# One attention-plus-MoE kernel: the route of its first loads, the written order of its first steps, and the form of its slot table

## The chip, the cores and the metric

The kernel runs on one core of a Trainium2 chip. The metric is device time in microseconds (us), the median of several executions. Before the change it is 366.8 us (three runs, 366.43 to 367.79). The profile was taken in an execution of its own, of 357.85 us, whose span from first to last instruction is 356.3 us. Sums of durations are made against that span.

The engines are TensorE (PE, with its weight loads listed as PEld), VectorE (DVE), ScalarE (ACT), GpSimd (POOL) and SyncE (SP). DMAs are issued by SP, ACT and POOL.

## The reference

There are two stages. The second takes the rows of the first.

```
q_n = q / sqrt(mean(q*q) + 1e-6) * g_q          # per row of 64, likewise k_n
attn = softmax(q_n @ k_n^T / 8)                 # 8 batches, 12 heads, 448 tokens
x = (attn @ v)  as rows [3584, 768]
e(row) = token_id * 2654435761 % 8              # expert of each row, from its low 3 bits
out[row] = relu(x[row] @ w1[e]) @ w2[e]         # w1: 8 x 768 x 1024, w2: 8 x 1024 x 768
```

## The kernel before

**Attention.** Two heads make one step, so that a batch has six steps and the whole has 48 (0 to 47). Steps are prepared in groups: batch 0 has groups of one, two and three steps, every later batch two groups of three. Groups are numbered 0 to 16 (0, 1, 2 are batch 0; 3 and 4 are batch 1).

Preparing a group consists of these operations, named as in the written order: `sqq`/`sqk` (squares of q and k, on DVE or, for two of them, ACT), `sumq`/`sumk` (16 matmuls against the identity that fold the squares), `redq`/`redk` (row sums on DVE), `ln` and `er` (on ACT, giving one over the root), `nk:g.h`/`nq:g.h` (DVE multiplies half a group by it), `v` (a DVE copy of v into the tile `v8`, which also has a column of ones).

A step consists of `Tk`/`Tq` (four PE transposes each, into two halves of one PSUM tile `qkT_ps`, of which there is one), `kT`/`qT` (DVE empties each half), `sc:s.j` (scores, j = 0 to 3, into three PSUM tiles), `exp:s.j` (ACT, PSUM to SBUF), `av:s.0` to `av:s.2` (PE, against v8), `rec` and `x` (DVE: reciprocal of the row sums and the product). When a batch is done its x goes to a DRAM scratch.

The order of all these is written out by hand as two strings of tokens: one for everything up to the first score of step 9 and around it, one (`steady`) that is repeated for each later group. Every engine executes its own instructions in the order in which the tokens emit them. An access to a tile waits for the earlier conflicting accesses to that tile in this same emitted order. `spin` tokens are dummy matmuls on a zero tile, `warm`. `zero:n` tokens are memsets of the parts of q, k, v and v8 buffers that no load fills.

**Loads.** POOL's queue carries nearly all loads; each converts fp32 in DRAM to 16 bits in SBUF. A load of q is two DMAs, one of k or v four. Only the first step's q and k (tile `first`, laid over an exp buffer, fp32) go over SP and ACT, q ahead of k. Then POOL issues: the identity; q, k, v of the rest of batch 0; batch 1 in two halves with a memset of `k_bufs[1]` between and one of `q_bufs[1]` behind; batch 2 with a memset of `v_bufs[1]`; the constants of `setup2`; batch 3. Later batches, and the expert weights, are issued from `hooks(s)`, which runs behind `x` of step s-1.

**Slot table.** While attention runs, the rows of experts 0 and 1 get slots. `SIDE[s]` puts small DVE pieces (m1 to m12) behind `x` of step s-1, and `AV_SIDE[s]` puts pieces of PE work, with a DVE piece that reads them, inside the `av` of step s; these use the free end of that step's `av_ps` bank. The table itself is m10a: 28 matmuls, one per column of tokens, each with a 128x32 stationary tile `lo` and a 128x30 moving tile `hi`, all into partitions 0 to 31 of the bank. The result is the index tile `gidx`, used by the row gathers at the end of attention.

**MoE.** Eight experts follow, two GEMMs each, 512 slots per expert; rows are gathered from and scattered to DRAM by POOL. This part is not touched.

Of the kernel before, what the change touches and what calls it, by code (L numbers as in the profile page):

```python
# [11 lines left out]
I32 = mybir.dt.int32  # L12
AF = mybir.ActivationFunctionType
# [6 lines left out]
def kernel(  # L20
# [12 lines left out]
    nc = tc.nc  # L33
# [63 lines left out]
    iota_i = consts.tile([P, P], I32)  # L97
# [10 lines left out]
    hv = consts.tile([P, 2 * HI0, NTC], FP16)  # L108
    lv = consts.tile([P, LO0, NTC], FP16)
# [5 lines left out]
    warm = consts.tile([P, 512], FP16)  # L115
# [12 lines left out]
    def setup2():  # L128
# [30 lines left out]
        G.tensor_copy(tv16[:], tv[:])  # L159
# [69 lines left out]
    with tc.manual_schedule(), \  # L229
# [21 lines left out]
            :, 0:4 * 8 * D].bitcast(FP32).rearrange("p (a n s d) -> p a n s d", a=2, n=1, d=D)  # L251
# [36 lines left out]
        def raw(a, gi):  # L288
            return first[:, a] if gi == 0 else part_of((q_bufs, k_bufs)[a], *groups[gi])
# [82 lines left out]
        excl = rt([P, 2, NTC], BF16, "excl")  # L372
        far = rt([P, NTC], FP32, "far")
        offl = rt([P, 2], FP32, "offl")
        mine = rt([P, 2, NTC], FP32, "mine")
        slot = rt([P, NTC], I32, "slot")
        parts = rt([P, 2, NTC], I32, "parts")
        parts_h = rt([P, 2, NTC], FP16, "parts_h")
        hi = rt([P, 2 * HI0, NTC], FP16, "hi")
        lo = rt([P, LO0, NTC], FP16, "lo")  # L380
        emp = rt([P, 2 * HI0], FP32, "emp")
        pos = rt([P, 2 * HI0], FP32, "pos")
        flat = lambda t: t[:].rearrange("p a c -> p (a c)")

        def m1():
            V.tensor_scalar(out=eid[:], in0=tid32[:, :, 0], scalar1=E - 1, scalar2=None,
                            op0=ALU.bitwise_and)
            V.tensor_copy(eidf[:], eid[:])

        def m2():  # L390
            for e in range(2):
                V.tensor_scalar(out=oh[:, e], in0=eidf[:], scalar1=float(e), scalar2=None,
                                op0=ALU.is_equal)
            V.tensor_tensor_scan(flat(incl), flat(keep), flat(oh), 0.0, op0=ALU.mult, op1=ALU.add)

        def m3():
            V.tensor_scalar(out=far[:], in0=oh[:, 1], scalar1=-3.0 * FAR, scalar2=4.0 * FAR,
                            op0=ALU.mult, op1=ALU.add)
            V.tensor_tensor(out=excl[:], in0=incl[:], in1=oh[:], op=ALU.subtract)
            V.scalar_tensor_tensor(out=far[:], in0=oh[:, 0], scalar=-4.0 * FAR, in1=far[:],  # L400
                                   op0=ALU.mult, op1=ALU.add)

        SP = SL * (D + 1)

        def m4a(av):
            nc.tensor.matmul(av[:, SP:SP + 2], lhsT=emask[:], rhs=incl[:, :, NTC - 1],
                             start=False, stop=True, skip_group_check=True)

        def m4b(av):
            V.tensor_scalar(out=offl[:], in0=av[:, SP:SP + 2], scalar1=float(EARLY),  # L410
                            scalar2=late[:], op0=ALU.max, op1=ALU.mult)

        def m4c(av):
            rank = av[:, SP:SP + 2 * NTC]
            nc.tensor.matmul(rank, lhsT=u128[:], rhs=flat(oh), start=False, stop=False,
                             skip_group_check=True)
            nc.tensor.matmul(rank, lhsT=gmask[:], rhs=flat(excl), start=False, stop=True,
                             skip_group_check=True)

        def m4d(av):  # L420
# [6 lines left out]
        def m5():  # L427
            V.tensor_tensor(out=far[:], in0=mine[:, 0], in1=far[:], op=ALU.add)
            V.tensor_tensor(out=slot[:], in0=mine[:, 1], in1=far[:], op=ALU.add)

        def m6():
# [4 lines left out]
            V.tensor_copy(parts_h[:], parts[:])  # L436
# [4 lines left out]
        def m7():  # L441
            V.tensor_tensor(out=hi[:], in0=hv[:], in1=wide(parts_h[:, 0], 2 * HI0),
                            op=ALU.is_equal)

        def m8():
            V.tensor_tensor(out=hi[:], in0=hi[:], in1=wide(tv16, 2 * HI0), op=ALU.mult)

        def m9():
            V.tensor_tensor(out=lo[:], in0=lv[:], in1=wide(parts_h[:, 1], LO0), op=ALU.is_equal)

        def m10a(av):
            for c in range(NTC):
                nc.tensor.matmul(av[0:LO0, SP:SP + 2 * HI0], lhsT=lo[:, :, c], rhs=hi[:, :, c],
                                 start=False, stop=(c == NTC - 1), skip_group_check=True)

        def m10b(av):
            val = av[0:LO0, SP:SP + 2 * HI0]
            e1, p1 = emp[0:LO0], pos[0:LO0]
            V.tensor_scalar(out=e1, in0=val, scalar1=0.0, scalar2=float(BIG),
                            op0=ALU.is_equal, op1=ALU.mult)  # L460
            V.tensor_copy(p1, val)

        def m11():
            e1, p1 = emp[0:LO0], pos[0:LO0]
            V.scalar_tensor_tensor(out=p1, in0=p1, scalar=float(N // 2), in1=e1,
                                   op0=ALU.add, op1=ALU.add)
            V.tensor_scalar(out=e1, in0=p1, scalar1=float(N // 2), scalar2=-1.0,
                            op0=ALU.is_gt, op1=ALU.mult)

        def m12():  # L470
            by = lambda t, g: t[0:LO0].rearrange("p (e h) -> p e h", e=2)[:, :, g::NL]
            for g in range(NL):
                n = len(range(g, HI0, NL))
                V.tensor_tensor(
                    out=gidx[LO0 * g:LO0 * g + LO0, 0:2 * KT].rearrange(
                        "p (e c) -> p e c", e=2)[:, :, 0:n],
                    in0=by(pos, g), in1=by(emp, g), op=ALU.add)
# [138 lines left out]
        def ones_v8(eng, v8):  # L616
            eng.memset(v8[:, :, 0:3, D:DP], 1.0)
            eng.memset(v8[:, :, 4:7, D:DP], 1.0)
            eng.memset(v8[:, :, 3::4, D:DP], 0.0)
            eng.memset(v8[0:64, :, 3, D:DP], 1.0)  # L620
            eng.memset(v8[64:P, :, 7, D:DP], 1.0)

        def zeros(n):
            return warm[:, None, 0:D].to_broadcast([P, n, D])

        def zero_act(t, n0, n1, slots):
            for p0, s in slots:
                nc.scalar.copy(t[p0:p0 + 64, n0:n1, s, :], zeros(n1 - n0)[p0:p0 + 64])

        def zero(part):  # L630
            V = nc.vector
            if part == 0:
                zero_kv(V, first[:, 1], 0, 1)
                zero_q(V, first[:, 0], 0, 1)
# [5 lines left out]
            elif part == 3:  # L640
                zero_kv(V, v_bufs[0], 0, 2 * HP)
            elif part == 4:
                for v8 in v8_tiles:
                    ones_v8(V, v8)
            else:
                zero_act(k_bufs[0], HP, 2 * HP, ((64, 3), (0, 7)))
                zero_act(q_bufs[0], HP, 2 * HP, ((64, 3), (64, 7)))

        load_q([nc.sync, nc.scalar], first[:, 0], 0, 0, 1)
        load_kv([nc.sync, nc.scalar, nc.sync, nc.scalar], first[:, 1], k, 0, 0, 1)  # L650
        setup()
        nc.vector.memset(warm[:], 0.0)
# [4 lines left out]
        load(1, 0, 3, "kqv")  # L657
        zero_kv(nc.gpsimd, k_bufs[1], 0, 2 * HP)
        load(1, 3, 3, "kqv")
        zero_q(nc.gpsimd, q_bufs[1], 0, 2 * HP)  # L660
# [15 lines left out]
        AV_SIDE = {16: (m4a, m4b), 18: (m4c, m4d), 28: (m10a, m10b)}  # L676
        SIDE = {13: m1, 14: m2, 15: m3, 19: m5, 20: m6, 22: m7, 24: m8, 26: m9, 29: m11, 30: m12}
# [44 lines left out]
        def emit(text, g, s):  # L722
# [12 lines left out]
            zero:2 zero:5 zero:0 sqk:0 zero:1 sqq:0 spin:9 sumq:0 zero:4 redq:0 zero:3 spin:4  # L735
            sumk:0 redk:0 ln:0 sqq:1 gain:0 er:0 nk:0.0 nk:0.1 spin:4 sumq:1 sqk:1 nq:0.0 spin:1
            Tk:0 nq:0.1 spin:1 sumk:1 redq:1 redk:1 ln:1 Tq:0 er:1 kT:0 qT:0 nk:1.0 spin:3 sc:0.0
            nk:1.1 nq:1.1 sc:0.1 nq:1.0 v:0 sc:0.2 exp:0.0 Tk:1 spin:1 Tq:1 sc:0.3 kT:1 exp:0.1
            exp:0.2 qT:1 sqk:2 spin:1 sc:1.0 Tk:2 exp:0.3 kT:2 Tq:2 exp:1.0 av:0.0 sc:1.1 sc:1.2
            qT:2 sqq:2 sumk:2 av:0.1 sc:1.3 exp:1.1 redk:2 sumq:2 exp:1.2 v:1 av:0.2 sc:2.0 v:2  # L740
            sc:2.1 exp:1.3 redq:2 sc:2.2 ln:2 rec:0 x:0 er:2 av:1.0 av:1.1 exp:2.0 exp:2.1 nk:2.0
            av:1.2 exp:2.2 nk:2.1 nq:2.0 nq:2.1 Tk:3 rec:1 sc:2.3 exp:2.3 Tq:3 kT:3 qT:3 x:1
            sqk:3 Tk:4 Tq:4 kT:4 sc:3.0 sc:3.1 qT:4 av:2.0 sumk:3 sqq:3 exp:3.0 redk:3 sc:3.2
            sc:4.0 sumq:3 av:2.1 sqk:4 exp:3.1 redq:3 sc:3.3 Tk:5 v:3 Tq:5 av:2.2 exp:3.2 exp:4.0
            ln:3 sc:4.1 kT:5 exp:3.3 sc:4.2 qT:5 sc:5.0 er:3 rec:2 exp:4.1 sumk:4 x:2 sc:4.3
            nk:3.0 exp:4.2 redk:4 exp:4.3 nk:3.1 nq:3.0 av:3.0 av:3.1 Tk:6 nq:3.1 sc:5.1 exp:5.0
            av:3.2 kT:6 rec:3 Tq:6 qT:6 sc:5.2 exp:5.1 sc:5.3 x:3 sc:6.0 v:4 exp:5.2 Tk:7 kT:7
# [351 lines left out]
```

## Time and profile before

| what | value |
|---|---|
| median time | 366.8 us |
| span of the profiled execution | 356.3 us |
| busy share PE / DVE / ACT / POOL | 94% / 63% / 53% / 49% |
| first `exp` starts | 13.10 us |
| step 9 starts (`exp:9.0`) | 48.73 us |
| last `exp` ends | 172.02 us |
| first MoE GEMM starts | 174.51 us |
| steady spacing of `exp` steps with no wait | 2.82 us |

The busy shares are means over two stages: attention to about 172 us, in which ACT has the exponentials, and the MoE stage behind it, in which PE is busy all the time (30.00 of 30 us in each stretch from 200 to 320 us). An ACT row of the timeline gives the start, the duration of a merged run of instructions and, in brackets, the idle time ahead of it with the engine that ended it.

### The profile page before, as it was taken

How to read it: one execution, taken by the hardware profiler on the slowest of the kernel's cores; microseconds unless marked ns; L12 is line 12 of the kernel's file. 1: busy time of each engine (PE TensorE's matmuls, PEld its weight loads, DVE VectorE, ACT ScalarE, POOL GpSimd, SP SyncE). 2: the span in 40 equal slices, each digit the busy share in tenths (PEclk: the TensorE clock that was granted, in tenths of full speed). 3: DMA queues.
4: the chain of work that ended last, by engine and by line, in shares of the span. 5: the costliest groups of instructions: out<-in, count | busy, mean ns of one | idle time of the engine just before them, and what ended most of it. 6: DMA issues, size and time to landing. Idle time of an engine off the chain costs nothing. (4 is left out here: it accounts for less than half of the span.)

```text
span 356.3 us, 9342 instructions
## 1 busy us (share of the span) xinstructions
PE 334.6 (94%) x3882; PEld 233.2 (65%) x3882; DVE 223.2 (63%) x574; ACT 188.3 (53%) x293; POOL 174.6 (49%) x253
## 2 busy tenths in 40 slices
PE   6888999999999999999898999999999999999992
PEld 3465667677677677765776767767676676766761
DVE  4888799999998999986788753233233223323311
ACT  4598789999998899999432220202211111111210
POOL 8899996564654210003155258736547374303122
PEclk9999899999999999999999999999999999999998
DMA  8999959999999999952479996999999999702012
GB/s 126 150 141 139 178 108 164 231 193 230 194 230 200 221 240 224 236 100 84 114 157 198 273 227 137 264 247 240 257 198 268 231 233 254 253 3 118 31 63 99
DMA packets 54449, 64.60 MB, mean 181 GB/s; under 512 B 22739, under 2 KB 42459, under 8 KB 54020
## 3 DMA queue, kind: packets, MB, share of 16 engines
q0 software_dynamic: 50832, 57.98, 88.1%
q1 hardware_dynamic: 2978, 5.44, 5.2%
q10 hardware_dynamic: 594, 0.56, 0.5%
q8 instruction: 31, 0.51, 0.5%
q14 instruction: 14, 0.11, 0.1%
HBM read 89.29 MB, written 17.30 MB: 299 GB/s over the span
## 5 line engine op out<-in xcount | busy, mean ns | idle before, releaser
L527 ACT ACTIVATE expT<-sc_ps 128x896 bf16<-128x896 f32 x144 | 123.2, 943 | 6.6 <-PE sc_ps L512 6.4
L805 PEld LDWEIGHTS <-h_sb 128*128 128x128 f16 (+1 forms) x512 | 51.2, 104 | 30.2
L805 PE MATMUL o_ps<-w_sb,h_sb 128*128 128x512 f16 (+3 forms) x384 | 66.2, 326 | 0.0
L812 POOL DMA_INDIRECT out_dram<-o_sb,gidx x32 | 32.6, 1020 | 60.6 <-ACT o_sb L811 27.0
L793 ACT ACTIVATE h_sb<-h_ps 128x480 f16<-128x480 f32 (+2 forms) x44 | 21.8, 498 | 72.0 <-PE h_ps L789 67.7
L203 POOL DMA_INDIRECT xg<-x_scratch,gidx x32 | 32.3, 1011 | 55.2 <-issue 35.4
L789 PEld LDWEIGHTS <-w_sb 128*128 128x128 f16 x336 | 44.2, 146 | 15.3 <-issue 1.1
L789 PE MATMUL h_ps<-xT,w_sb 128*128 128x480 f16 x240 | 49.6, 366 | 0.0
L811 ACT COPY o_sb<-o_ps 128x768 f32<-128x768 f32 x16 | 12.8, 798 | 69.1 <-PE o_ps L805 69.1
L795 DVE TENSOR_SCALAR h_sb<-h_ps 128x480 f16<-128x480 f32 x28 | 18.4, 656 | 42.6 <-PE h_ps L789 42.6
L512 PE MATMUL sc_ps<-qT,kT 64*128 64x448 f16 x288 | 42.4, 359 | 2.5 <-DVE qT L504 0.8
L544 PEld LDWEIGHTS <-expT 128*128 128x128 bf16 x864 | 36.5, 98 | 8.1 <-DVE x_sb L577 6.6
L544 PE MATMUL av_ps<-v,expT 128*128 128x65 bf16 x864 | 41.0, 194 | 0.7 <-DVE x_sb L577 0.5
L811 DVE COPY o_sb<-o_ps 128x768 f32<-128x768 f32 (+1 forms) x16 | 15.3, 956 | 35.4 <-PE o_ps L805 31.1
L494 PE MATMUL qkT_ps<-ident,n 128*128 128x128 f16 x384 | 31.0, 220 | 4.1 <-DVE kT L501 2.0
L270 POOL DMA_DIRECT2D kr<-in_k_dram x40 | 25.8, 657 | 14.6 <-DMA qr<-in_q_dram 9.7
L494 PEld LDWEIGHTS <-n 128*128 128x128 f16 x384 | 22.2, 97 | 15.8 <-issue 10.8
L215 DVE COPY xT<-xT_ps 128x768 f16<-128x768 f16 x28 | 15.5, 553 | 25.4 <-PE xT_ps L214 25.4
L320 PEld LDWEIGHTS <-ident 128*128 128x128 f16 x544 | 24.6, 98 | 9.2 <-issue 4.4
L577 DVE TENSOR_TENSOR x_sb<-av_ps,srec 128x448 f16<-128x448 f32 x48 | 29.8, 620 | 1.2
L530 ACT ACTIVATE expT<-sc_ps 128x448 bf16<-128x448 f32 x48 | 28.2, 588 | 1.5 <-PE sc_ps L515 1.5
L270 POOL DMA_DIRECT2D vr<-in_v_dram x40 | 25.9, 668 | 4.8 <-DMA kr<-in_k_dram 4.0
(186 smaller groups left out, 491.3 us busy)
## 6 DMA issues: line engine op xcount, KB each, us to landing
w_sb<-in_moe_w_dram POOLq DMA_DIRECT2D x24, 384.0 KB, 11.3
w_sb<-in_moe_w_dram POOLq DMA_DIRECT2D x8, 768.0 KB, 12.3
x_scratch<-x_sb SPq DMA_DIRECT2D x15, 288.0 KB, 6.1
w_sb<-in_moe_w_dram POOLq DMA_DIRECT2D x2, 1536.0 KB, 24.0
qr<-in_moe_w_dram POOLq DMA_DIRECT2D x8, 384.0 KB, 17.6
kr<-in_k_dram POOLq DMA_DIRECT2D x12, 192.0 KB, 7.8
qr<-in_q_dram POOLq DMA_DIRECT2D x6, 384.0 KB, 7.7
vr<-in_v_dram POOLq DMA_DIRECT2D x12, 192.0 KB, 9.5
```

Source lines behind the costliest of these rows:

```text
L203: nc.gpsimd.indirect_dma_start(out=xg[0:idx.shape[0]], out_offset=None, in_=x_dram[0:rows, :], in_offset=bass.IndirectOffsetOnAxis(ap=idx, ...
L270: eng.dma_start(out=dst[64 * half:64 * half + 64, :, s0:s0 + cnt, :].rearrange("p n s d -> p n (s d)"), in_=runs(t, h0 + hh, 2, n, tok0, s ...
L494: nc.tensor.transpose(T[:, o:o + P], n8[:, a, i, j].rearrange("p h d -> p (h d)"), ident16[:])
L512: nc.tensor.matmul(sc[:, hh, :S], lhsT=kT[64 * hh:64 * hh + 64, P * j:P * j + P], rhs=qT[64 * hh:64 * hh + 64, :], start=True, stop=True)
L527: nc.scalar.activation(expT[:, 2 * j:2 * j + 2, :], sc[:, :, :S], AF.Exp, bias=0.0, scale=1.0)
L530: nc.scalar.activation(expT[:, 6, :], sc[:, 0, :S], AF.Exp, bias=0.0, scale=1.0)
L544: nc.tensor.matmul(av[:, 2 * t + hh, :], lhsT=expT[:, tl(hh, j), P * t:P * t + P], rhs=v8[:, i, 4 * hh + j, 0:D + 1], start=(hh == 0 and t ...
L577: nc.vector.tensor_tensor(out=xs[b][:, :, hp * D:hp * D + D], in0=av[:, :, :D], in1=srec[:, :, None].to_broadcast([P, SL, D]), op=ALU.mult)
L789: nc.tensor.matmul(h_ps[:, :c1 - c0], lhsT=w1v[:, co, fo, :], rhs=xT[:, co, c0:c1], start=(co == 0), stop=(co == CO - 1))
L805: nc.tensor.matmul(o_ps[0:w, d0:d1], lhsT=h_sb[:, fo, col * P:col * P + w], rhs=w2_sb[:, fo, d0:d1], start=(fo == 0), stop=(fo == FO - 1))
L811: (nc.vector.tensor_copy if col % 2 else nc.scalar.copy)(o_sb[0:w], o_ps[0:w])
L812: scat = nc.gpsimd.indirect_dma_start(out=out[:, :], out_offset=bass.IndirectOffsetOnAxis(ap=idx[0:w], axis=0), in_=o_sb[0:w], in_offset=N ...
```

## The change

- The first step's q is loaded by POOL's queue, as its first DMAs, into `q_bufs[0]` with conversion. Its k alone uses SP and ACT and the tile `first`.
- Batch 1 is loaded whole: k, q, v, ten DMAs in place of twenty. The memsets of `k_bufs[1]` and `q_bufs[1]` move from POOL to DVE (`zero:4`, `zero:5`).
- `v8` gets its ones column with three memsets in place of five, each of one column in place of four.
- The two order strings are replaced.
- The slot table's pieces are rewritten (m1 to m14): 16-bit integer slots without a cast, a base added to the offsets in place of the `far` tile, the wide compares halved and one half per step (23 to 28), and two tables (occupied, and position) of 28 matmuls each in steps 29 and 31. Matmul c writes to partition group 32*(c mod 4), four column tiles of the array. Two matmuls with a replicated identity (`rep4`) combine them in step 33.
- `setup2` makes the new constants (`ug`, `base2`, `rep4`); `iota_i` and `warm` are laid over `lo` and `hi`.

```diff
-    hv = consts.tile([P, 2 * HI0, NTC], FP16)
-    lv = consts.tile([P, LO0, NTC], FP16)
+    hv = consts.tile([P, 2 * HI0, NTC], I16)
+    lv = consts.tile([P, LO0, NTC], I16)
+    rep4 = consts.tile([P, 2, NL, LO0], FP16)
...
-        def m10a(av):
-            for c in range(NTC):
-                nc.tensor.matmul(av[0:LO0, SP:SP + 2 * HI0], lhsT=lo[:, :, c], rhs=hi[:, :, c],
-                                 start=False, stop=(c == NTC - 1), skip_group_check=True)
+        def m13a(av, a):
             for c in range(NTC):
+                g = LO0 * (c % NL)
+                nc.tensor.matmul(av[g:g + LO0, SP:SP + 2 * HI0], lhsT=lo[:, :, c],
+                                 rhs=hi[:, a, :, c], start=False, stop=(c >= NTC - NL),
+                                 skip_group_check=True)
...
         def zero(part):
...
+            elif part == 4:
+                zero_kv(V, k_bufs[1], 0, 2 * HP)
+            elif part == 5:
+                zero_q(V, q_bufs[1], 0, 2 * HP)
...
-        load_q([nc.sync, nc.scalar], first[:, 0], 0, 0, 1)
-        load_kv([nc.sync, nc.scalar, nc.sync, nc.scalar], first[:, 1], k, 0, 0, 1)
+        load(0, 0, 1, "q")
+        load_kv([nc.sync, nc.scalar, nc.sync, nc.scalar], first, k, 0, 0, 1)
...
-        load(1, 0, 3, "kqv")
-        zero_kv(nc.gpsimd, k_bufs[1], 0, 2 * HP)
-        load(1, 3, 3, "kqv")
-        zero_q(nc.gpsimd, q_bufs[1], 0, 2 * HP)
+        load(1, 0, HP)
...
-        AV_SIDE = {16: (m4a, m4b), 18: (m4c, m4d), 28: (m10a, m10b)}
-        SIDE = {13: m1, 14: m2, 15: m3, 19: m5, 20: m6, 22: m7, 24: m8, 26: m9, 29: m11, 30: m12}
+        AV_SIDE = {17: (m5a, m5b), 19: (m7a, m7b), 33: (m14a, m14b)}
+        for a in range(2):
+            AV_SIDE[29 + 2 * a] = (lambda av, a=a: m13a(av, a), lambda av, a=a: m13b(av, a))
+        SIDE = {13: m1, 14: m2, 15: m3, 16: m4, 18: m6, 20: m8, 21: m9}
+        for t, m in enumerate((m10, m10, m11, m11, m12, m12)):
+            SIDE[23 + t] = lambda m=m, e=t % 2: m(e)
...
-            Tk:0 nq:0.1 spin:1 sumk:1 redq:1 redk:1 ln:1 Tq:0 er:1 kT:0 qT:0 nk:1.0 spin:3 sc:0.0
+            Tk:0 nq:0.1 sqk:1 kT:0 spin:1 Tq:0 spin:1 sumk:1 qT:0 sc:0.0 redk:1 ln:1 sc:0.1
+            zero:5 er:1 nk:1.0 exp:0.0 sc:0.2 nk:1.1 nq:1.0 spin:5 Tk:1 nq:1.1 spin:1 Tq:1 v:0
...
-            av:3.2 kT:6 rec:3 Tq:6 qT:6 sc:5.2 exp:5.1 sc:5.3 x:3 sc:6.0 v:4 exp:5.2 Tk:7 kT:7
-            Tq:7 qT:7 av:4.0 av:4.1 av:4.2 sc:7.0 sqq:4 exp:5.3 exp:6.0 sc:6.1 sc:6.2 sumq:4
+            qT:6 exp:5.2 sc:5.3 exp:5.3 av:4.2 sc:6.0 Tk:7 Tq:7 sc:6.1 sc:6.2 sqq:4 rec:4 x:4
+            kT:7 qT:7 av:5.0 v:3 exp:6.0 sqk:5 sc:6.3 av:5.1 sumq:4 exp:6.1 av:5.2 sc:7.0 redq:4
```

## The prediction, made before the run

> **What bounds the kernel now.** I read the page first (busy shares), then the table of stretches, ACT's waits and the timeline. The chain of waits shows only the last scatter, so the bound has to be read by stage.
>
> ```profile
> PE 334.6 (94%) x3882; PEld 233.2 (65%) x3882; DVE 223.2 (63%) x574; ACT 188.3 (53%) x293; POOL 174.6 (49%) x253
> ...
> 31.00:38.90 7.90, 6.50 (x99) 4.63 (x97) 6.62 (x16) 5.16 (x9) 7.85 (x12) 0.85 1.21 145
> 38.90:48.73 9.83, 9.14 (x157) 6.29 (x154) 8.15 (x18) 8.48 (x14) 8.93 (x32) 0.95 1.11 171
> ...
> 89.74:98.91 9.17, 9.07 (x166) 6.40 (x163) 9.10 (x23) 9.13 (x15) 5.82 (x10) 1.00 1.51 192
> 98.91:108.84 9.93, 9.44 (x170) 6.71 (x166) 9.69 (x24) 9.31 (x16) 5.91 (x9) 1.00 1.42 227
> 108.84:120.06 11.22, 11.15 (x194) 8.41 (x192) 9.20 (x26) 9.45 (x14) 4.90 (x8) 1.00 1.30 208
> ```
>
> Behind each stretch stand its length and the busy time of PE, PEld, DVE, ACT, POOL. A steady group takes about 9.1 us, and ACT is busy for all of it (9.13 of 9.17); groups that take longer are those in which ACT waits. From 172 us on PE is the bound and no PE row waits for a weight DMA. So a microsecond that ACT no longer waits in attention is a microsecond at the end, and there is nothing to gain elsewhere.
>
> How much is there? A step of `exp` is 2.82 us (starts at 160.42, 163.23, 166.04), `ln` with `er` 0.62, the one square on ACT 1.50. Up to step 9 ACT needs 9 x 2.82 + 3 x 0.62 + 1.5 = 28.8, and takes 13.10 to 48.73 = 35.6: 6.9 us of waits. From there to 172.02 it needs 39 x 2.82 + 12 x 0.62 = 117.4 and takes 123.3: 5.9 us. These 12.8 us are all that the change can work on, besides the start at 13.10.
>
> ```profile
> 38.90 2.54 ACT L527 ACTIVATE expT<-sc_ps 128x896 bf16<-128x896 f32 x3 [2.35 <-PE sc_ps L512]
> 48.73 2.54 ACT L527 ACTIVATE expT<-sc_ps 128x896 bf16<-128x896 f32 x3 [1.07 <-PE sc_ps L512]
> ...
> 34.93 0.91 DVE L361 COPY v<-vr 128x1536 bf16<-128x1536 bf16 x1
> 35.76 0.46 DVE L501 TENSOR_SCALAR kT<-qkT_ps,g_col 128x512 f16<-128x512 f16 x1
> 36.28 0.38 PE L494 MATMUL qkT_ps<-ident,n 128*128 128x128 f16 x4 [1.01 <-DVE kT L501]
> 38.24 1.30 PE L512 MATMUL sc_ps<-qT,kT 64*128 64x448 f16 x6
> ...
> 113.96 1.85 PEld L453 LDWEIGHTS <-lo 128*32 128x32 f16 x28
> 116.26 0.54 ACT L530 ACTIVATE expT<-sc_ps 128x448 bf16<-128x448 f32 x1 [1.49 <-PE sc_ps L515]
> 108.84 0.34 ACT L335 ACTIVATE ss<-ss,eps_col 128x48 f32<-128x48 f32 x1 [0.43 <-DVE ss L331]
> ```
>
> The largest wait (2.35) is one of order: `v:4` holds DVE for 0.91, `kT:7` comes behind it, `Tq:7` is emitted behind `kT:7` on the same tile and waits 1.01, three `av` follow, and only then the scores that ACT wants. The granted clock is also low there (0.85). The last two rows are the slot table: 28 matmuls in series (66 ns each) make ACT wait 1.49; DVE pieces ahead of `redq` make each `ln` wait, 0.2 to 0.7 us a group (70.75, 89.74, 108.84).
>
> **What the Trainium skill says.** "TensorEngine Tiling (Array Packing)", Key Properties: different tiles can execute weight loads and matmuls in parallel. The trace agrees in kind: the eight matmuls of `av:s.2`, two column halves, load their weights in 0.20 us, 25 ns each, against 66 ns in the unpacked table. "DMA: Bandwidth & Descriptors", Issuing engines are not separate DMA queues: SP, ACT and POOL share the same DMA engines; so moving q to POOL buys issue order, not bandwidth. The trace can't separate that. "GPSIMD Engine Reference", Key points: POOL shares its SBUF interfaces with VectorE. It agrees: the v copy under POOL's memset took 0.91, others 0.55. "VectorE: DVE Perf Modes", What auto-detection actually checks: the doubled rate asks for 16-bit tensors, so int16 compares should keep the 0.58 us rate of the fp16 ones; no int16 row is in this trace.
>
> **The change part by part.**
>
> *First loads.*
>
> ```profile
> 0.97 0.20 POOL masks.py:197 MEMSET ident<- 128x128 f16 x1 [0.29 <-POOLq L1083]
> 1.72 0.83 POOL L260 DMA_DIRECT2D qr<-in_q_dram  x1 [0.18 <-issue]
> 4.36 0.69 DVE L308 TENSOR_TENSOR sq_q<-expT 128x512 f16<-128x512 f32 x1 [1.28 <-DMA expT<-in_q_dram]
> 7.25 0.63 ACT L306 ACTIVATE sq_k<-expT 128x512 f16<-128x512 f32 x1 [0.20 <-DMA expT<-in_k_dram]
> 8.74 0.31 ACT L335 ACTIVATE ss<-ss,eps_col 128x16 f32<-128x16 f32 x1 [0.87 <-DVE ss L331]
> ```
>
> On POOL the first q can be issued at about 0.97 and 1.80; POOL's q issues of that size landed 4.4 to 4.7 us later, so q is there at 6.2 (before: 4.36). k, now first on SP and ACT, has its second pieces issued at 1.8 and 4.2 to landing: 6.0 (before 7.25). DVE then: `sqq:0` on fp16 (half the elements of the 0.68 us row, 0.4), nine small memsets (before, fifteen took 1.28; I take 0.8), `zero:4` 0.76, `redq`, `redk` 0.35: 8.5. `ln:0` at 8.5 in place of 8.74. POOL's later issues slip by the two of q, 1.4 us: q of group 1 lands at 3.9 + 4.4 = 8.3, in time for `sqq:1`; its k at 6.3 + 4.0 = 10.3. `sqk:1` stands ahead of `kT:0` on DVE and ends at 11.1, `kT:0` at 11.5; `Tq:0` is now emitted behind `kT:0` and waits for it, 12.0; `sumk:1` (0.63) stands ahead of the first score; `ln:1` and `er:1` (0.6) stand ahead of `exp:0.0` on ACT. So `exp:0.0` starts at about 13.6, a loss of 0.5. Bounds: 12.9 if the loads land a little earlier, 14.6 if POOL's land a microsecond later. `zero:5` (twice the 0.38 row) lies in the wait for `er:1`: nothing.
>
> *Batch 1 whole.* Ten issues fewer at 0.64 (6.4 us) and three memsets (0.73 + 0.73 + 1.68) leave POOL; `setup2` gains about nine small operations (0.2 to 0.5 each, some 2.5 us). No engine waits for a POOL constant, so this is worth nothing by itself, but for the one DMA wait of `sq_k` (0.81 at 27.72), which ends on DVE and not on ACT. What must hold is that whole k lands before `sqk:3` on ACT, at about 24. The queues had moved 0.97, 1.16 and 1.27 MB in the stretches of 8 us to 24; batch 0 and all k of batch 1 are 2.95 MB: 21 to 22 us. In time.
>
> *Order to step 9.* Of the 6.9 us of waits: `exp:1.1` (0.69) stays, as `sc:1.1` is still behind `Tq:2` behind `kT:2` behind `sqk:2`. `ln:2` (0.42) shrinks, since `v:2` (half of a 1.08 us pair) leaves its place ahead of `redq:2`. The 2.35 goes: `Tk:7 Tq:7 sc:6.1 sc:6.2` follow each other and `Tq:7` waits for no `kT`. The 1.07 goes: `exp:8.1` to `8.3` (2 us) now stand between the last `av:7` and `exp:9.0`. For step 6, DVE has 3.5 us of work between `er:3` and `qT:6`, ACT 4.9 us of `exp`: no wait. I keep 2.5 us of 6.9 for what I can't see: step 9 at 13.6 + 28.8 + 2.5 = 44.9, 3.8 us earlier. Bounds: 1 and 6 of waits.
>
> *Slot table and steady order.* Of 5.9 us, 1.5 is the table and about 4.4 the waits at group borders. DVE loses the casts, `far` and the two passes at the end (about 1.5 us), and gains nearly as much by halving wide passes (fixed cost twice); but a border now has at most one piece of 0.1 to 0.35 ahead of it in place of 0.4 to 0.6: I take 2.6 for 4.4. The table is 56 matmuls for 28, in two steps. Packed at 25 ns each half takes 0.7, of which PE's slack (1.85 - 1.49 = 0.4) hides 0.4: 0.6 in all, for 1.5. Unpacked it is 2 x 1.5 = 3.0; fully hidden 0. Sum: 2.6 + 0.6 against 5.9, 2.7 us earlier; between 0.3 and 4.
>
> Sum: 3.8 + 2.7 = 6.5 us earlier at the end of attention, and at the end: 356.3 - 6.5 = 349.8 in the profiled execution. The others were 10 us longer, with no profile to say where; I take the same difference from the median: 366.8 - 6.5 = 360.3.
>
> **The rivals.**
> 1. *The column tiles don't pack.* The slow 66 ns may be the strided weight read, which stays. Then the table costs 3.0 in place of 0.6, and the steady part gives little: 362.5 to 364. For it: the trace shows packing only with 64 columns. Against: there it works.
> 2. *The order gains nothing that can be measured.* Waits removed at one step come back at the next, because PE and DVE are busy 9 of 9.1 us in a steady group and have no room; the start loses 0.5 to 1. Then 365 to 367. Against: up to 48 us both have room (6.5 and 6.6 of 7.9 us).
> 3. *Slower: whole k comes late.* `sqk:3` holds ACT, in order, so each microsecond past 24 is lost. In the crowded stretch at 60 to 80 us POOL's k issues were 1.5 to 2 us apart and landed 7.8 us later. At that pace the last of four from 15.6 lands at 29.4: 5.4 us lost, q behind it, `sqq:3` too. It outweighs the gain if k lands past 32, with the median then at 369. Against: the bytes moved by 24 us, above.
> 4. *The first q late on POOL* is a matter of 1 us and within the range.
>
> **How the numbers follow.** Likeliest 0.60: 360.3, own range 357 to 363. Rival 1, 0.17: 363.3. Rival 2, 0.11: 366. Slower (rival 3 or its like), 0.12: 369. A measurement of this kernel tells about 0.5%, 1.8 us, from no change. Faster 0.77, same 0.11, slower 0.12. The range is 357.0 to 366.0: it leaves out rival 3, and the few cases below 357 in which nearly all 12.8 us of waits go.
>
> **What would show it.** Right: `exp:0.0` between 13 and 14.5; no ACT wait above 1 us between 20 and 45; step 9 near 45; granted clock near 1 there; two runs of 28 table matmuls of about 0.7 us; last `exp` near 165.5; the MoE stage as long as before. Wrong: an ACT wait at `sqk:3` for a DMA, table runs of 1.9 us each, `exp:0.0` past 15, or a MoE stage that grows by what attention gave.

## The result, and the profile after

The changed kernel took 360.77 us in the median (359.99 to 361.48, four runs), the kernel before 366.93 us (366.43 to 367.79, four runs): ratio 0.983, 95% interval 0.980 to 0.986. The predicted time was 360.3.

The profile does not bear out that difference. The profiled execution of the kernel before had a span of 356.3 us, that of the changed kernel 359.7. Three later sessions, on three different chips, put the kernel before at 359.2 to 359.3 us (166 executions, none above 361.7), and the changed kernel, run in two of them, at the same. The first comparison stands as measured, but what the change does has to be read from traces and from the later comparisons.

The busy shares and five stretches of the changed kernel (columns as before: bounds, length, then busy time of PE, PEld, DVE, ACT, POOL):

```profile
PE 334.4 (93%) x3911; PEld 232.4 (65%) x3911; DVE 225.6 (63%) x567; ACT 187.4 (52%) x293; POOL 170.6 (47%) x250
```

```profile
31.00:38.90 7.90, 7.57 (x129) 5.10 (x126) 7.13 (x19) 7.55 (x13) 7.31 (x20) 1.00 1.51 194
38.90:47.32 8.42, 7.61 (x145) 5.66 (x144) 8.20 (x18) 7.57 (x12) 7.81 (x22) 1.00 0.79 142
89.71:99.03 9.32, 9.32 (x168) 6.50 (x164) 9.22 (x25) 9.07 (x14) 5.73 (x9) 1.00 1.51 193
99.03:108.68 9.65, 9.48 (x166) 6.59 (x164) 9.55 (x25) 9.07 (x15) 5.91 (x9) 1.00 1.42 228
108.68:118.68 10.00, 9.80 (x192) 7.18 (x192) 9.38 (x24) 9.19 (x14) 4.36 (x8) 1.00 1.34 203
```

Up to step 9 the order does its work: between 31.00 and 38.90 ACT is busy for 7.55 us, where it was 5.16, and the granted clock is 1.00, where it was 0.85. The stretch with the table is 10.00 us, where it was 11.22. But the two steady stretches together are hardly shorter than before (18.97 us for 19.10).

The timeline of the changed kernel, ACT's waits and what stands behind them:

```profile
13.86 2.51 ACT L533 ACTIVATE expT<-sc_ps 128x896 bf16<-128x896 f32 x3
47.32 2.57 ACT L533 ACTIVATE expT<-sc_ps 128x896 bf16<-128x896 f32 x3 [0.38 <-PE sc_ps L518]
52.72 0.34 ACT L344 ACTIVATE ss<-ss,eps_col 128x48 f32<-128x48 f32 x1 [2.38 <-DVE ss L340]
117.71 0.54 ACT L536 ACTIVATE expT<-sc_ps 128x448 bf16<-128x448 f32 x1 [0.38 <-PE sc_ps L521]
171.45 0.57 ACT L536 ACTIVATE expT<-sc_ps 128x448 bf16<-128x448 f32 x1
...
49.11 2.54 DVE L370 COPY v<-vr 128x1536 bf16<-128x1536 bf16 x1
49.15 2.09 POOL L668 MEMSET xg<- 128x768 f16 x3
52.43 0.25 DVE L340 TENSOR_REDUCE ss<-qkT_ps 128x24 f32<-128x96 f32 x1
...
116.73 0.53 PEld L463 LDWEIGHTS <-lo 128*32 128x32 f16 x28
116.73 0.65 PE L463 MATMUL av_ps<-hi,lo 128*32 128x30 f16 x28
...
174.87 5.04 PE L796 MATMUL h_ps<-xT_e,w_sb 128*128 128x384 f16 x30 [0.98 <-DVE xT_e L224]
222.02 0.49 PE L223 MATMUL xT_ps<-ident,xg 128*128 128x128 f16 x6 [1.42 <-DVE xT L224]
```

Step 9 starts at 47.32 (before 48.73), although the first `exp` starts 0.76 later. Then one wait of 2.38 us takes it back: the copy `v:4`, 0.55 us in other steps, takes 2.54 while POOL runs three memsets, and `redq` stands behind it on DVE. The table packs: 28 weight loads in 0.53 us, ACT's wait 0.38 in place of 1.49. The last `exp` ends at 172.02 in both kernels. The MoE stage (from its first GEMM to the end of the span) takes 184.8 us, before 181.8; PE has waits in it that the kernel before doesn't have (1.42 at 222.02, 0.52 at 214.56, 0.42 at 181.48; the 0.98 ahead of the first GEMM is as before).

Three questions remain: does the change gain, which of its parts cost what it gives, and why is the MoE stage longer?

### The profile page after: what moved, and what is told of

It reads as the page before. It is cut to its first block, busy times and chain, and to the rows that moved or that the text cites. A ratio compares the mean times of both kernels' runs of the same rounds, so it can differ in the third digit from the quotient of the medians.

```text
span 359.7 us, 9392 instructions
## 1 busy us (share of the span) xinstructions
PE 334.4 (93%) x3911; PEld 232.4 (65%) x3911; DVE 225.6 (63%) x567; ACT 187.4 (52%) x293; POOL 170.6 (47%) x250
## 5 line engine op out<-in xcount | busy, mean ns | idle before, releaser
L212 POOL DMA_INDIRECT xg<-x_scratch,gidx x32 | 32.5, 1015 | 56.1 <-DVE qT L510 28.6
L550 PEld LDWEIGHTS <-expT 128*128 128x128 bf16 x864 | 36.6, 97 | 17.1 <-DVE x_sb L583 13.3
L518 PE MATMUL sc_ps<-qT,kT 64*128 64x448 f16 x288 | 44.0, 356 | 1.7 <-DVE qT L510 0.8
L550 PE MATMUL av_ps<-v,expT 128*128 128x65 bf16 x864 | 43.4, 193 | 2.0 <-DVE x_sb L583 1.9
L279 POOL DMA_DIRECT2D kr<-in_k_dram x36 | 23.3, 662 | 19.0 <-DMA qr<-in_q_dram 13.3
L329 PEld LDWEIGHTS <-ident 128*128 128x128 f16 x544 | 25.4, 99 | 4.9 <-issue 3.2
L279 POOL DMA_DIRECT2D vr<-in_v_dram x36 | 23.3, 675 | 5.4 <-DMA kr<-in_k_dram 4.1
```

Source lines behind the costliest of these rows:

```text
L212: nc.gpsimd.indirect_dma_start(out=xg[0:idx.shape[0]], out_offset=None, in_=x_dram[0:rows, :], in_offset=bass.IndirectOffsetOnAxis(ap=idx, ...
L279: eng.dma_start(out=dst[64 * half:64 * half + 64, :, s0:s0 + cnt, :].rearrange("p n s d -> p n (s d)"), in_=runs(t, h0 + hh, 2, n, tok0, s ...
L518: nc.tensor.matmul(sc[:, hh, :S], lhsT=kT[64 * hh:64 * hh + 64, P * j:P * j + P], rhs=qT[64 * hh:64 * hh + 64, :], start=True, stop=True)
L550: nc.tensor.matmul(av[:, 2 * t + hh, :], lhsT=expT[:, tl(hh, j), P * t:P * t + P], rhs=v8[:, i, 4 * hh + j, 0:D + 1], start=(hh == 0 and t ...
```

## The experiments

Medians in us, each beside the kernel before of its own session (359.2 to 359.3). "New loads and order" means the first loads, batch 1 whole and both order strings.

| kernel | loads and order | batch 1 | slot table | median | ratio to before, 95% interval |
|---|---|---|---|---|---|
| b_again | old | halves | old | 359.66 | 0.999 to 1.004 |
| whole_b1_only | old | whole | old | 359.12 | 0.997 to 1.000 |
| table_only | old | halves | new | 363.72 | 1.007 to 1.017 |
| table_whole_b1 | old | whole | new | 358.36 | 0.995 to 0.999 |
| order_only | new | whole | old | 357.88 | 0.995 to 0.999 |
| a_again, a_third | new | whole | new | 359.23, 359.28 | 0.997 to 1.002, 0.999 to 1.002 |

Five more kernels, told further down, move the xg memsets or pad PE's instructions.

**The two kernels again (b_again, a_again, a_third).** No edit.

> The kernel before, unchanged, profiled a second time. Its first profile (span 356.3 us) is 10 us shorter than its other runs (366.8), and step 9 started at 48.73, the last exp ended at 172.02. Theory A (the 6 us are the ACT waits that the prediction counts): this profile has the same waits, the last exp ends near 172, and the 10 us lie behind it. Theory B (the first profile is not a typical execution): the last exp ends 5 to 10 us later than 172, with waits on ACT that the first profile doesn't have. Ratio to itself 1.00.

> The changed kernel, unchanged, profiled a second time. Theory A: last exp near 172 as in its first profile, time 361. Theory B: also 172; it is the kernel before that moves. If its own last exp moves by more than 2 us between profiles, the executions differ by chance and one profile of each kernel can't be compared.

> The changed kernel again, beside the one before. The recorded pair had 366.9 before and 360.8 after; the second pair 359.2 and 359.2. If the difference of 6 us belongs to the change, the ratio is near 0.983 here too; if it belongs to the chip or the session that ran the first pair, it is near 1.00, with both near 359.

The changed kernel and the kernel before agree on two chips (ratios 0.999 and 1.001). The spans of three profiled executions of the changed kernel are 356.7, 357.8 and 359.7, of the kernel before 356.3 and 359.4. So the first gain of 6 us is not repeated. No execution of about 367 us was profiled, so what lengthened the kernel before in that session stays open.

The second profile of the kernel before also shows how far two traces of one kernel can differ. Its last `exp` ends at 175.20, 3.2 us later than in the first, and ACT has two waits just behind step 9 that the first trace doesn't have. The memsets and the copy in b_again, those two waits, and then the same memsets and the same copy in the first trace:

```profile
50.04 2.08 POOL L666 MEMSET xg<- 128x768 f16 x3
50.06 2.48 DVE L361 COPY v<-vr 128x1536 bf16<-128x1536 bf16 x1
53.60 0.34 ACT L335 ACTIVATE ss<-ss,eps_col 128x48 f32<-128x48 f32 x1 [1.94 <-DVE ss L331]
58.30 2.53 ACT L527 ACTIVATE expT<-sc_ps 128x896 bf16<-128x896 f32 x3 [1.19 <-PE sc_ps L512]
...
47.86 2.08 POOL L666 MEMSET xg<- 128x768 f16 x3
50.06 0.55 DVE L361 COPY v<-vr 128x1536 bf16<-128x1536 bf16 x1
```

In the first trace the memsets end 0.1 us before the copy begins, in b_again they begin just ahead of it. So the kernel before can meet the same collision of memsets and v copy, and the wait of 2.38 above is not a cost that only the change has. Sums that are read from single traces carry this spread of up to 3 us.

**The slot table alone, and the loads and order alone.** table_only takes from the change the pieces m1 to m14, their steps and their constants; order_only takes all the rest.

```diff
-        AV_SIDE = {16: (m4a, m4b), 18: (m4c, m4d), 28: (m10a, m10b)}
+        AV_SIDE = {17: (m5a, m5b), 19: (m7a, m7b), 33: (m14a, m14b)}
...
+            G.tensor_copy(rep4[r, 1], ident16[r, None, r].to_broadcast([LO0, NL, LO0]))
```

(table_only, against the kernel before; order_only is the reverse edit, against the changed kernel.)

> The kernel before with the new slot table alone (its constants, its pieces and their steps), loads and order as before. The prediction's sum gives 2.7 us of 6.5 to table and steady order: ratio about 0.994 to 0.997 if it is additive. A rival, that the whole gain is the order and the loads: ratio 1.000. A rival, that the whole gain is the table: 0.983.

> The changed kernel with the old slot table: new loads, new memsets, new order, old table pieces and their old steps. The prediction: 3.8 us of start plus part of the borders, ratio about 0.987 to 0.990. If the whole gain is the table: 1.000. If the gain is all order and loads: 0.983.

The table alone makes the kernel 4.5 us slower (ratio 1.012, 1.007 to 1.017), which no expectation allowed for; the loads and order without it gain 1.35 us (0.997, 0.995 to 0.999), less than the 0.987 to 0.990 expected. The table's own matmuls pack here too. What costs is seen in the timelines of DVE and POOL in table_only:

```profile
40.68 0.30 POOL L131 IOTA lo<- 128x128 int32 x1
53.76 0.53 POOL L172 TENSOR_SCALAR base_e<-iota_f 128x8 f32<-128x8 f32 x1
54.24 2.09 POOL L672 MEMSET xg<- 128x768 f16 x3
56.28 2.70 POOL L279 DMA_DIRECT2D kr<-in_k_dram  x4
...
64.82 0.96 DVE L317 TENSOR_TENSOR sq_k<-kr 128x1536 f16<-128x1536 f16 x1 [5.17 <-DMA kr<-in_k_dram]
65.98 0.34 ACT L344 ACTIVATE ss<-ss,eps_col 128x48 f32<-128x48 f32 x1 [5.36 <-DVE ss L340]
```

The constants take 13.6 us on POOL (40.68 to 54.24); in b_again they took 10.1 (39.97 to 50.04). Behind them on POOL's queue stand the loads of batch 3. Their first is issued at 56.28, in b_again at 52.08, and DVE waits 5.17 us for k. If that is the cause, anything that takes 5 us off POOL ahead of the constants must repair it.

**Batch 1 whole, with the new table and without.**

```diff
-        load(1, 0, 3, "kqv")
+        load(1, 0, HP)
         zero_kv(nc.gpsimd, k_bufs[1], 0, 2 * HP)
-        load(1, 3, 3, "kqv")
```

> The kernel before with the new slot table, as in table_only, and with batch 1 loaded whole; steps and first loads as before. Theory: table_only lost 4.5 us because its constants hold POOL some 6 us longer, and the loads of batch 3 stand behind them on POOL's queue: DVE waited 5.2 us for k at 64.8. Loading batch 1 whole takes ten issues (6.4 us) off POOL ahead of the constants, so that wait should go and the median fall to 359 to 360.5. Rival: the table's own pieces on DVE and PE are what costs in the old order; then it stays near 363.7.

> The kernel before with batch 1 loaded whole, and nothing else. The prediction priced this at nothing by itself. With the old constants POOL had time to spare (before has no wait of DVE for k at step 12), so 358.5 to 359.5, within 0.3% of before. If the ten issues taken off POOL are worth something even there, as the 5.4 us between table_only and table_whole_b1 let one think, 357 to 358.

table_whole_b1 drops from 363.72 to 358.36, and in its trace the constants begin at 34.01, the loads of batch 3 at 48.62, and DVE doesn't wait for k:

```profile
34.01 0.30 POOL L131 IOTA lo<- 128x128 int32 x1
48.62 2.80 POOL L279 DMA_DIRECT2D kr<-in_k_dram  x4
58.98 0.95 DVE L317 TENSOR_TENSOR sq_k<-kr 128x1536 f16<-128x1536 f16 x1
```

Without the new table the same edit gives 359.12 (0.997 to 1.000): nothing. So the same ten issues are worth nothing, or 5.4 us (two sessions, whose kernels before differ by 0.06), according to whether the loads behind them are late.

These two kernels also give the new order its price. With the new table and batch 1 whole, old loads and order stand at 358.36, new ones at 359.28. The start costs: first `exp` at 13.0 to 14.5 in the six traces with old loads (mean 13.7), 13.8 to 15.0 in the eight with new ones (mean 14.5). Up to step 9 the order pays: from first `exp` to step 9 the six traces with the old order take 34.2 to 36.6 us (mean 35.1), the eight with the new one 32.5 to 33.5 (mean 32.8). Behind step 9 it loses again: from there to the last `exp` table_whole_b1 takes 121.5 us, with four waits of `ln` of 0.2 to 0.4, a_third 123.7, with a wait of 1.35 behind the v copy and eight waits of 0.3 to 0.6. Where the new order doesn't meet the memsets (after_xg_moved, below) it takes 122.3.

**The memsets of xg.** Three memsets of 0.7 us each, behind the constants on POOL, are not needed before the gathers at about 163. Here they move from behind `setup2` to `hooks(s)` at step 36; POOL then runs them at 117.83 to 119.94, where no v copy was slowed:

```diff
-        for xg in xg_e:
-            nc.gpsimd.memset(xg[:], 0.0)
+            if s == 36:
+                for xg in xg_e:
+                    nc.gpsimd.memset(xg[:], 0.0)
```

> The changed kernel, with the three memsets of xg (2.09 us on POOL) moved from behind the constants to step 36. Theory: they stretch the v copy on DVE from 0.55 to 1.4 or 2.5 us just ahead of a redq, and make ln wait 1.4 to 2.4 us at 52; without them the copy takes 0.55, that wait is under 0.6, the loads of batch 3 are issued 2 us sooner, and the last exp and the end come 1 to 2 us sooner: 357.5 to 358.5 where the changed kernel has 359.2. Rival: the wait comes back at a later step or in the MoE stage: 359.2.

> The changed loads and order with the old slot table, and the memsets of xg moved to step 36. In order_only the memsets ran at 45.8 to 47.9 and met the v copy at 46.88 (1.38 for 0.55) with no wait of ACT behind it, so the collision theory expects no more than 0.5 us here: 357.4 to 357.9, the same as order_only. If it gains over 1 us, sooner loads are what counts, not the collision.

On the changed kernel: 357.77 (0.995 to 0.998), 1.5 us less than a_third in the same session. DVE and ACT of its trace, at the place of the 2.38:

```profile
49.09 0.56 DVE L370 COPY v<-vr 128x1536 bf16<-128x1536 bf16 x1
50.71 0.34 ACT L344 ACTIVATE ss<-ss,eps_col 128x48 f32<-128x48 f32 x1 [0.39 <-DVE ss L340]
```

The copy is back at 0.56 and `ln` waits 0.39. With the old table the same move gives 358.20 (0.996 to 0.999), no gain over order_only's 357.88: there the slowed copy was `v:3`, at 46.88, and the waits of ACT that followed were small (0.65 at 49.97, 0.50 at 51.02). That supports the collision, and not the sooner loads, as the cause; so does b_again, where nothing was edited.

**The longer MoE stage.** In the old-table traces the MoE stage takes 181.7 to 182.7 us, in the unpadded new-table traces 183.0 to 184.8. This is where it parts. POOL's gathers in a_third (the fourth reads the last batch's rows), then PE:

```profile
178.25 1.00 POOL L212 DMA_INDIRECT xg<-x_scratch,gidx  x1 [0.30 <-issue]
180.59 1.00 POOL L212 DMA_INDIRECT xg<-x_scratch,gidx  x1 [1.34 <-DVE offl L921]
...
214.24 0.51 PE L223 MATMUL xT_ps<-ident,xg 128*128 128x128 f16 x6 [1.81 <-DMA xg<-x_scratch,gidx]
```

The fourth gather waits 1.34 us. The engine named is only the latest event; the gather needs the store of x, and the DMA issues of a_third show that store landing late. Of a DMA issue the last two columns are its size and the us from issue to landing:

```profile
x_scratch<-x_sb ACTq DMA_DIRECT2D x1, 288.0 KB, 4.4
x_scratch<-x_sb ACTq DMA_DIRECT2D x1, 48.0 KB, 5.5
```

The queue table of a_third from 176.59 to 178.59 (packets, MB, share of 16 engines' time):

```profile
q0 software_dynamic: 59, 0.18, 33.0%
q10 hardware_dynamic: 124, 0.20, 31.4%
q1 hardware_dynamic: 79, 0.05, 8.2%
q8 instruction: 1, 0.02, 2.9%
```

With the old table the 48 KB store lands after 4.3 to 4.4 us, with the new one, unpadded, after 5.5 to 5.6 (in the five traces that show it). In these 2 us a queue that fetches instructions moves one packet of 16 KB. The packets' own times in the trace: the fetch runs from 3.31 to 4.22 us behind the first MoE GEMM; of the small packets on SP's queue q1 all but four start by 3.45, the last four at 4.22 to 4.43; likewise four on q10. The store's 64 packets are four for each of 16 engines, so this reads as one DMA engine held for 0.9 us; the records don't name the engine. (A second fetch queue, q14, moves a packet of 8 KB at 3.25; it does so at 3.26 in after_pad too, where the store isn't late.) In all six unpadded new-table traces this fetch comes at 3.3; in the five old-table traces at 6.5 to 7.2, when the store is done. So the table would cost here by the number of instructions on PE (the change adds 29 matmuls). The test changes that number, in the `spin` matmuls before the first scores, and leaves their work as it was (450 columns for 448):

```diff
-            for _ in range(cnt):
-                nc.tensor.matmul(wps[:, 0:448], lhsT=warm[:, 0:P], rhs=warm[:, 0:448],
+            for _ in range(3 * cnt):
+                nc.tensor.matmul(wps[:, 0:150], lhsT=warm[:, 0:P], rhs=warm[:, 0:150],
```

> The changed kernel with each warming matmul of 448 columns written as three of 150: 46 more instructions on PE, the same work, all of them before the first scores. Theory: a fetch of PE's instructions (16 KB on one DMA engine, 0.9 us) falls 3.3 us after the first MoE matmul in every kernel with the new slot table, and holds the last four packets of the x store on that engine (landing 5.5 in place of 4.4 us); the gather of the last batch, the weights and, at about 214, PE come 1 to 1.8 us late. The 46 instructions move that fetch some 5 us sooner, to where no store runs: landing 4.4, the fourth gather 5.5 us after the MoE start, PE's wait for xg at 214 under 0.5, and 358.0 to 358.6 where the changed kernel has 359.28. Rival: the wait is the table's own doing (its index order, or the gathers); then nothing moves: 359.3.

> The same pad on after_xg_moved (memsets of xg at step 36). Theory: the two gains add, 1.5 us of the memsets and about 1 of the fetch: 356.5 to 357. Rival: they share one slack, and it stays at 357.7.

> The same pad (here 48 more instructions) on table_whole_b1: old first loads and old order, new slot table, batch 1 whole. Theory: PE's wait for xg (0.93 at 211) goes, 358.36 becomes 357.2 to 357.6, and that is no slower than the changed kernel with the same pad, so the new order and first loads gain nothing. If the new order is worth something, it stays over 1 us behind after_pad.

after_pad takes 357.63 us (0.994 to 0.998), 1.65 less than a_third on another chip, where the kernel before differs by 0.08. Its store; the queue table from 171.50 to 172.50, where the fetch now is (1.65 us ahead of the first GEMM); and the gathers and PE:

```profile
x_scratch<-x_sb ACTq DMA_DIRECT2D x1, 48.0 KB, 4.4
```

```profile
q8 instruction: 1, 0.02, 6.7%
```

```profile
177.78 1.00 POOL L212 DMA_INDIRECT xg<-x_scratch,gidx  x1 [0.30 <-issue]
179.09 1.01 POOL L212 DMA_INDIRECT xg<-x_scratch,gidx  x1 [0.30 <-issue]
...
212.54 0.51 PE L223 MATMUL xT_ps<-ident,xg 128*128 128x128 f16 x6 [0.53 <-DMA xg<-x_scratch,gidx]
```

The landing is 4.4 again, the gather follows without a gap, and PE's wait falls from 1.81 to 0.53; the MoE stage takes 182.3 us, in a_third 183.7. That step of the chain is shown, though the pad moves every later fetch as well. The pad gains in the other kernels too: old_order_pad 357.48 (0.993 to 0.997), 0.88 less than table_whole_b1, and best_pad_xg 357.13 (0.991 to 0.996), 0.64 less than after_xg_moved. The two gains don't add in full (357.13, expected 356.5 to 357). In best_pad_xg PE still waits 0.87 at 212.42 with its store landing in 4.4, so that wait has a second source, which stays open. best_pad_xg is the fastest version run: 0.7% ahead of the kernel before. With the same pad old and new order are equal (357.48 and 357.63).

## Why the prediction was right in its number and wrong in its working

The predicted 360.3 and the measured 360.77 agree, and the range and the direction held for the recorded pair. That agreement is luck, and not evidence for the working. The working said that the profiled span falls by 6.5 us, to 349.8; it was 359.7. The step "I take the same difference from the median" joined a span to timed runs 10 us longer "with no profile to say where". In those runs, which no profile shows, lies the recorded gain; in the later sessions neither they nor the gain came back.

- *First loads.* Predicted `exp:0.0` at 13.6, a loss of 0.5. Measured 13.86, within its bounds; over all traces the new loads cost 0.8 (14.5 for 13.7, with traces of one kernel up to 1.4 apart). q was issued at 1.53 and not at 0.97. Right in kind, a little too mild.
- *Order to step 9.* Predicted 44.9, measured 47.32. The two large waits went as said: no wait above 1 us between 20 and 45. But of the waits 4.7 us stayed, where 2.5 were kept: an `exp` of step 1 still waited 1.12 (at 19.43), and `ln:2` 0.75, where less than 0.42 was expected. The term was mis-sized by 2.2 us.
- *Slot table.* Right: packed, 28 matmuls in 0.65 us (0.7 predicted), ACT's waits 0.38 and 0.39 for 1.49. The int16 compares ran at the rate of the fp16 ones, 0.37 us a half. Rival 1 falls.
- *Steady order.* Failed. 4.4 us of border waits were to become 2.6, and with the table's 0.6 the stretch from step 9 to the last `exp` was to take 120.6 us. The three traces of the changed kernel take 123.7 to 124.7, the two before 123.3 and 126.5. Even without the memset collision the changed kernel takes 122.3 (after_xg_moved), so about 4.9 us of waits stay, where 3.2 were expected. table_whole_b1 and old_order_pad, with the old strings, take 121.5 and 121.4: the new table gains there, and the new steady string loses about 1 us of it. Rival 2, an order that gains nothing in sum, was the better forecast; its reason, that DVE has no room, was not tested.
- *Batch 1 whole.* "No engine waits for a POOL constant, so this is worth nothing by itself" was true of the edit by itself (359.12), and missed the other half: loads stand behind those constants. `setup2` grew by 3.5 us (10.1 in b_again, 13.6 in table_only) where 2.5 were allowed, and without the ten issues saved this costs 5.4 us. Nor was the collision of the memsets behind `setup2` with a v copy priced, though the prediction quoted such a slow copy (0.91 at 34.93); it took 2.54, and moving the memsets away gave 1.5 us. b_again shows that the kernel before pays this too in some executions.
- *MoE as long as before.* Failed: 184.8 for 181.8 in the first traces, 183.0 to 184.8 for 181.7 to 182.7 over all. No rival had a mechanism for it, though a longer MoE stage stands among the signs of being wrong. About 1.4 us of it (183.7 to 182.3, a_third and after_pad) is an instruction fetch that meets the store of x.
- *Rivals 3 and 4.* Whole k of batch 1 was in time: no wait of ACT at `sqk:3`. The late q on POOL was within the range.

So the change gives about 2.3 us up to step 9 and 2 by the table behind it (from step 9 to the last `exp` 123.5 us in whole_b1_only, 121.5 in table_whole_b1), and pays 0.8 at the start, about 1 for the steady string, 0.6 to 1.65 for the fetch (the three pairs with and without the pad), and up to 1.5 for the v copy, which the kernel before pays at times too. These are estimates from single traces and from medians of different sessions; their sum is within about 1 us of nothing, and so are the medians (a_third 1.0006, 0.9988 to 1.0023).

## What to carry to other kernels

A POOL instruction costs what is queued behind it: ask not only who waits for its result, but which loads it holds back, and when they are needed. When a profiled span and the timed runs of the same kernel differ by more than the effect that is looked for, run the kernel before again before a mechanism is believed. And a kernel whose stage grows without one of its instructions being changed may have had its instruction fetches moved: look at what else runs on the DMA engines in that microsecond.

## What the runs showed of the hardware that was not expected

- A fetch of PE's instructions shows as a DMA packet of 16 KB that took 0.9 us (a_third, 3.31 us behind the first MoE GEMM). The last four packets of a store in flight started only when it had ended, as if it held one of the 16 DMA engines: 48 KB landed in 5.5 in place of 4.4 us. 46 more PE instructions moved the fetch by 5 us.
- POOL's memsets stretched a 128x1536 DVE copy from 0.55 to 1.4 (a_third) and 2.54 us (the changed kernel's first trace), more than the 0.91 seen before. In all six traces in which a v copy met the xg memsets it ended 0.42 us after the last of them, whether it had begun with the first memset (2.48 and 2.54 us) or 1.1 us behind it (1.38 to 1.40 us). So the copy looks to be held until the memsets end, and not merely slowed.
- Four column groups of 32 took 28 weight loads of a 128x32 tile from 1.85 to 0.53 us, though the loads are strided.
